# New priorities for a list-scheduled attention and mixture kernel

## The chip, the cores and the metric

The kernel runs on one core of a Trainium2 chip. The metric is device time in microseconds, the median of a few runs. The engines named here are TensorE (PE: matmuls and transposes), VectorE (DVE), ScalarE (ACT), GpSimd (POOL) and SyncE (SP, which issues the DMAs).

## The reference

The inputs are q, k and v for 8 batches, 8 heads, 576 positions and head size 64. For each head the scores q·kᵀ/8 are formed, every score below its row's maximum less tau (0.02) is dropped, the softmax of the rest is taken and multiplied by v. The heads of a batch together are x, 576 positions by 512 channels. Then:

```
theta = x @ w_theta
y = w_tok_r @ (x * cos(theta)) + w_tok_i @ (x * sin(theta))
u = x + y
out = u + relu(u @ w_ch)
```

w_theta and w_ch are 512 by 512, w_tok_r and w_tok_i are 576 by 576. Some weights come in 64-bit floats, and each weight is split into a high and a low 32-bit part; matmuls are done in three terms (high by high, high by low, low by high) to keep the precision.

## The kernel before, in words

**Tiling.** Heads are taken in pairs, 4 pairs to a batch and 32 in all. A pair has 9 *units* (288 in all, numbered h): 128 query rows of one head, or in the pair's first unit the last 64 rows of both heads. A unit is a chain over three engines. `score` (PE, L655) writes 128 by 576 scores into a PSUM tile of the kind "pair". `empty` (DVE, L670) scales them into a tile `sc` (4 of these exist) and takes the row extremum. `offset` (one small instruction) and `power` (ACT, the exponential, L691) follow. `mask` (DVE, L699) drops the small scores and sums the rows; it gives back the `sc` tile. `flip` (PE, L739) and `flip5` (L775) transpose the result, and `evict` (ACT, L750, L779) copies it out of PSUM. After the ninth unit `values` (PE, L823, 40 matmuls) multiplies by v, and `normalize` divides by the row sums, through a small DMA round trip (L865 to L883).

**The mixture.** When a batch has its four pairs, `mixture(b)` follows: `angle` (PE, L961, x by w_theta), `sines` (ACT, L1041), a multiplication on POOL (L1056; on DVE in the last batch), transposes (L1075), `token` (PE, L1123, the two token matrices, 216 matmuls), an addition (L1139), then the channel product (PE, L961 again, u by w_ch) and the store. It runs interleaved with the attention of the next batch; the last batch's mixture has nothing beside it.

**The weights.** At the start 13 pieces are loaded and split: 9 of the token matrices (576 wide, `weight_tok`) and 4 of w_theta (512 wide, `weight_mid`); 4 of w_ch follow after the first batch's scores. Each piece is one DMA, one ACT instruction (L348), five on DVE (L352, L356, L361, L366, L370), another on ACT (L375), matmuls into one or two banks (L399, L400) and ACT copies out (L403). Its tiles allow two pieces at a time. The token pieces are first read by `token(0)`, the w_theta pieces by `angle` of the first batch.

**What sets the order.** Nothing of this order is written out by hand. Every instruction, or small group of them, is a `Work` in a `Plan`: its engine, its modelled duration, what it needs, the buffers it takes, and a *rank*. When the program is built, `Plan.run` plays the whole list through. On the engine that can start something soonest it looks at all works that could start within a small slack of that moment (0.05 us on PE and POOL, 0.1 us on DVE and ACT, 0.8 us on SP) and takes the one with the lowest rank:

```
if first < NEVER and (best is None or first < best[0]):
    best = min((x for x in starts if x[0] <= first + SLACK[e]), key=lambda x: x[1].rank)
```

So the rank decides only between works that are ready together, and the program then issues each engine's instructions in the order found. A unit's rank is 3.2 h plus 3.2 times an entry of the table `LEAD`; in batch 0 the entry with a 0 behind its name is added (`score` and `score0`). A mixture's rank starts at 3.2 times 36 (b + 1), plus 3.2 times `mix`, and advances with its share of the mixture's matmuls. A token piece c has the rank 3.2 (`wk` + c `wk_step`), a w_theta piece 3.2 (`wt` + c `wt_step`). `prep` ranks the loads of q and k and their splitting, `wmload` the loads of the split w_theta and w_ch from DRAM. `split` is the time in us after which one of the two score tiles is given up for two more single banks. `angle`, `ztok`, `ztr`, `chan` and `span` set how fast a mixture's rank advances.

Of the kernel before, what the change touches and what calls it, by code (L numbers as in the profile page):

```python
# [39 lines left out]
SLACK = {"PE": 0.05, "DVE": 0.1, "ACT": 0.1, "POOL": 0.05, "SP": 0.8}  # L40

LEAD = dict(
    score=-4.72, empty=-32.86, offset=-8.97, power=-5.51, mask=15.23, flip=0.44, evict=-13.16, flip5=-0.53,
    values=1.44, vevict=-3.04, norm=-13.22, inv=-17.87, times=12.38, prep=-9.26, vload=3.1, mix=1.55, span=0.9,
    wt=0.48, wt_step=-10.83, wch=-3.05, wch_step=-0.24, wlow=14.42, xh=-17.5, xlast=15.0, angle=1.82, ztok=1.52,
    ztr=0.27, chan=0.95, aevict=4.03, wmload=6.36, absl=-8.83, sin=7.08, zmul=2.9, zev=-43.34, yev=-34.51, uh=-21.1,
    cev=-16.07, dma=1.13, hop=0.13, split=114.84, wk=-17.47, wk_step=-2.88, score0=-31.88, empty0=-6.42,
    offset0=15.77, power0=16.19, mask0=-7.4, flip0=-2.74, evict0=-0.54, flip50=-11.41, values0=-13.64,
    vevict0=-110.27, norm0=-7.09, prep0=-17.86, vload0=10.11, inv0=21.92, times0=17.78, mix0=-2.15, span0=0.08,
)  # L50


# [1211 lines left out]
```

## Time and profile before

| | us |
|---|---|
| median of 3 runs | 1006.82 |
| lowest, highest run | 1006.80, 1007.87 |
| span of the profiled execution, first to last instruction | 1003.4 |
| PE busy in it | 990.8 |
| DVE busy in it | 770.6 |
| ACT busy in it | 647.3 |
| POOL busy in it | 234.7 |

For the profiled execution only the span is listed, not its own time; the median lies 3.4 us above that span. The times of an engine are unions of its instructions. Those of PE are to be read with care: matmuls overlap each other and their ends are modelled, so a short wait may not show as idle time. The granted TensorE clock is full in every slice.

### The profile page before, as it was taken

To read this page: it belongs to the slowest core of one execution; us is meant where nothing else is said; L and a number is where in the kernel's file an instruction comes from. 1 tells how busy PE (TensorE), PEld (TensorE's weight loads), DVE (VectorE), ACT (ScalarE), POOL (GpSimd) and SP (SyncE) were. 2 spreads that over 40 slices of the span, in tenths; PEclk is the share of its full clock that TensorE was granted. 3 is DMA by queue.
4 is the path that set the end of the run, shared out by engine and by line. 5 is a ranking of instruction groups with operands and counts; after the bars stand their busy time and mean duration, and the time that the engine had idled before them with its cause. 6 is when DMAs were issued, how large, how long until landed. Compare 5 with 4: busy or idle time off the path is not lost.

```text
span 1003.4 us, 20961 instructions
## 1 busy us (share of the span) xinstructions
PE 990.8 (99%) x7574; PEld 890.5 (89%) x7574; DVE 770.6 (77%) x2038; ACT 647.3 (65%) x1292; POOL 234.7 (23%) x162
## 2 busy tenths in 40 slices
PE   9999999999999999999999999999999999999998
PEld 7766798998999989998999988999899989999898
DVE  7999978968866787767887688667887678876553
ACT  6898978645865568555775467755785457844430
POOL 2112132311342124222342113421242223400100
PEclk9999999999999999999999999999999999999999
DMA  7677946757534675437644575346853386441502
GB/s 227 201 208 193 245 154 170 201 150 218 163 88 101 189 218 133 118 72 231 183 126 103 144 203 166 98 107 164 236 141 90 85 241 188 110 92 34 174 22 69
DMA packets 86950, 151.89 MB, mean 151 GB/s; under 512 B 27200, under 2 KB 36672, under 8 KB 86848
## 3 DMA queue, kind: packets, MB, share of 16 engines
q1 hardware_dynamic: 86704, 150.56, 54.4%
q8 instruction: 60, 0.98, 0.4%
q14 instruction: 42, 0.34, 0.1%
q10 hardware_dynamic: 144, 0.00, 0.0%
HBM read 81.89 MB, written 13.78 MB: 95 GB/s over the span
## 4 chain that ended last, share of the span: by engine, by line
PE 91%; DVE 5%; issue 2%; DMA 1%; ACT 1%; SPq 0%; DVEq 0%; ACTq 0%
PE y_ps L1123 23%; PE m_ps L961 19%; PE o_ps L823 15%; PE s_ps L655 15%; PE t_ps L739 12%; PE z_ps L1075 3%; PE t_ps L775 2%; DVE s_sb L699 2%; DVE sc L670 1%; PE w_ps L399 1%; PE fill_ps L290 1%; DMA qraw<-in_qT_dram 0%; ACT a L750 0%; DMA wm<-wm_dram 0%; PE r_ps L854 0%
## 5 line engine op out<-in xcount | busy, mean ns | idle before, releaser
L670 DVE TENSOR_SCALAR_CACHE_REDUCE sc<-s_ps,small 128x576 f32<-128x576 f32 x288 | 234.0, 814 | 79.5 <-PE s_ps L655 78.2
L699 DVE SCALAR_TENSOR_TENSOR s_sb<-sc,nm,s_sb 128x576 f32<-128x576 f32 x288 | 241.7, 850 | 20.2 <-ACT s_sb L691 19.3
L691 ACT ACTIVATE s_sb<-sc,nm 128x576 f32<-128x576 f32 x288 | 222.6, 782 | 19.1 <-DVE sc L670 18.7
L750 ACT COPY a<-t_ps 128x512 f32<-128x512 f32 x256 | 150.3, 590 | 100.5 <-PE t_ps L739 99.3
L655 PE MATMUL s_ps<-kd,qq 128*128 128x288 f32 x992 | 179.1, 303 | 1.3 <-DVE sc L670 0.6
L739 PE MATMUL t_ps<-ident,s_sb 128*128 128x128 f32 x1152 | 173.3, 274 | 1.3 <-DVE s_sb L699 0.6
L1123 PE MATMUL y_ps<-wt_l,zh 128*128 128x288 f32 x576 | 166.6, 304 | 0.0
L1123 PE MATMUL y_ps<-wt_h,zh 128*128 128x288 f32 x576 | 166.4, 307 | 0.0
L823 PE MATMUL o_ps<-a,v 128*64 128x256 f32 (+1 forms) x1280 | 162.3, 408 | 0.0
L655 PEld LDWEIGHTS s_ps<-kd,qq 128*128 128x128 f32 x992 | 143.5, 188 | 7.0 <-DVE sc L670 5.5
L739 PEld LDWEIGHTS t_ps<-ident,s_sb 128*128 128x128 f32 x1152 | 137.1, 140 | 12.4 <-issue 7.9
L823 PEld LDWEIGHTS o_ps<-a,v 128*64 128x64 f32 x1280 | 89.1, 137 | 64.0 <-issue 3.9
L311 POOL TENSOR_TENSOR khl<-kraw,khl 128x576 fp32r<-128x576 f32 x31 | 47.3, 1526 | 325.1 <-ACT khl L551 206.5
L1056 POOL TENSOR_TENSOR z<-z,xT 128x576 f32<-128x576 f32 x56 | 78.2, 1431 | 138.0 <-ACT z L1041 138.0
L1123 PEld LDWEIGHTS y_ps<-wt_l,zh 128*128 128x128 f32 x576 | 108.2, 189 | 0.2
L1123 PEld LDWEIGHTS y_ps<-wt_h,zh 128*128 128x128 f32 x576 | 108.0, 189 | 0.3
L1123 PE MATMUL y_ps<-wt_h,zl 128*128 128x288 f32 x576 | 107.2, 298 | 0.0
L961 PE MATMUL m_ps<-xh,wm 128*128 128x288 f32 x512 | 97.4, 307 | 0.0
L961 PE MATMUL m_ps<-uh,wm 128*128 128x288 f32 x512 | 91.9, 302 | 0.9 <-DMA wm<-wm_dram 0.9
L1123 PEld LDWEIGHTS y_ps<-wt_h,zl 128*128 128x128 f32 x576 | 85.5, 188 | 0.4 <-issue 0.4
L834 ACT COPY xT<-o_ps 128x320 f32<-128x320 f32 x64 | 25.5, 398 | 93.3 <-PE o_ps L823 93.3
L961 PEld LDWEIGHTS m_ps<-xh,wm 128*128 128x128 f32 x512 | 75.5, 189 | 2.8 <-issue 2.7
(98 smaller groups left out, 1414.5 us busy)
## 6 DMA issues: line engine op xcount, KB each, us to landing
wm<-wm_dram SPq DMA_DIRECT2D x64, 512.0 KB
kd<-khl SPq DMA_DIRECT2D x62, 288.0 KB
qq<-qhl SPq DMA_DIRECT2D x124, 128.0 KB
kd<-khl SPq DMA_DIRECT2D x62, 256.0 KB
v<-in_vp_dram SPq DMA_DIRECT2D x32, 320.0 KB
kraw<-in_kT_dram SPq DMA_DIRECT2D x32, 288.0 KB
qraw<-in_qT_dram SPq DMA_DIRECT2D x32, 288.0 KB
rb<-rows_dram SPq DMA_DIRECT2D x64, 144.0 KB
```

The source lines that it names most:

```text
L311: eng.tensor_tensor(out=out, in0=a, in1=b, op=ALU.subtract)
L655: nc.tensor.matmul(ps.tile[:, half, to], st, kk[:, fr], start=(x == 0), stop=(x == len(terms) - 1))
L670: nc.vector.tensor_scalar(out=sc.tile.rearrange("p (a b) -> p a b", a=2), in0=ps.tile[:, :, :HS], scalar1=gate, scalar2=None, op0=ALU.mult ...
L691: nc.scalar.activation(out=u.s.tile[:, j], in_=sc.tile, func=AF.Exp, bias=nm.tile[:, 0:1], scale=-1.0)
L699: nc.vector.scalar_tensor_tensor(out=e, in0=sc.tile, scalar=nm.tile[:, 1:2], in1=e, op0=ALU.is_le, op1=ALU.mult, accum_out=pr.rows.tile[:, ...
L739: nc.tensor.transpose(out=bank.tile[:, c * P : (c + 1) * P], in_=sf[:, k0 + c * P : k0 + (c + 1) * P], identity=ident)
L750: nc.scalar.copy(out=t.a[:, :, j, q0 : q0 + P], in_=bank.tile.rearrange("p (c q) -> p c q", c=4))
L823: nc.tensor.matmul(bank.tile[64 * j : 64 * j + 64, :w], st, mv, start=(c == 0), stop=(c == 4))
L961: nc.tensor.matmul(banks[h].tile[:, :HS], wm.tile[:, a, c, :], x[:, h * HS : (h + 1) * HS], start=(key == 0), stop=(key == 11),)
L1056: eng.tensor_tensor(out=zi, in0=zi, in1=xs[m].x.tile, op=ALU.mult)
L1075: nc.tensor.transpose(out=bank.tile[:, i * P : (i + 1) * P], in_=z.tile[:, c : c + P], identity=ident)
L1123: nc.tensor.matmul(bank.tile[:, :HS], st, (wt_l if wl else wt_h)[:, c, hs], start=(k + q == 0), stop=(k + q == 26),)
```

## The change

Only the numbers of the table `LEAD` differ. The works, their needs, their modelled durations and their buffers are the same; the time at which the score tiles are split up (`split`) is one of the numbers.

```diff
 LEAD = dict(
-    score=-4.72, empty=-32.86, offset=-8.97, power=-5.51, mask=15.23, flip=0.44, evict=-13.16, flip5=-0.53,
-    values=1.44, vevict=-3.04, norm=-13.22, inv=-17.87, times=12.38, prep=-9.26, vload=3.1, mix=1.55, span=0.9,
-    wt=0.48, wt_step=-10.83, wch=-3.05, wch_step=-0.24, wlow=14.42, xh=-17.5, xlast=15.0, angle=1.82, ztok=1.52,
-    ztr=0.27, chan=0.95, aevict=4.03, wmload=6.36, absl=-8.83, sin=7.08, zmul=2.9, zev=-43.34, yev=-34.51, uh=-21.1,
-    cev=-16.07, dma=1.13, hop=0.13, split=114.84, wk=-17.47, wk_step=-2.88, score0=-31.88, empty0=-6.42,
-    offset0=15.77, power0=16.19, mask0=-7.4, flip0=-2.74, evict0=-0.54, flip50=-11.41, values0=-13.64,
-    vevict0=-110.27, norm0=-7.09, prep0=-17.86, vload0=10.11, inv0=21.92, times0=17.78, mix0=-2.15, span0=0.08,
+    score=-4.98, empty=-12.45, offset=-6.95, power=-1.14, mask=302.19, flip=0.97, evict=-106.74, flip5=0.33,
+    values=1.44, vevict=-44.01, norm=-20.15, inv=15.74, times=-60.18, prep=-6.6, vload=62.76, mix=1.4, span=0.9,
+    wt=-1.51, wt_step=-10.17, wch=11.16, wch_step=-14.85, wlow=-24.23, xh=-30.5, xlast=161.43, angle=1.743,
+    ztok=1.594, ztr=0.278, chan=0.926, aevict=-33.46, wmload=38.5, absl=56.98, sin=80.64, zmul=142.53,
+    zev=-188.21, yev=2.1, uh=-96.76, cev=-83.7, dma=1.13, hop=0.13, split=103.59, wk=-14.57, wk_step=2.97,
+    score0=-45.76, empty0=-58.68, offset0=17.08, power0=11.69, mask0=-60.05, flip0=-23.39, evict0=51.72,
+    flip50=-120.74, values0=102.45, vevict0=-21.98, norm0=-63.56, prep0=-20.42, vload0=-29.22, inv0=2.85,
+    times0=129.54, mix0=-0.37, span0=0.051,
 )
```

## Rows read from the trace of the kernel before

**Rows 1.** Stretches of the span: busy us (instructions) of each engine, clock, DMA.

```profile
17.00:117.00 100.00, 94.16 (x630) 70.79 (x630) 96.66 (x233) 90.23 (x216) 16.61 (x11) 1.00 0.75 208
...
117.00:144.70 27.70, 27.61 (x207) 24.01 (x207) 22.30 (x54) 21.04 (x46) 7.35 (x6) 1.00 0.64 172
...
125.00:875.00 750.00, 749.42 (x5872) 684.98 (x5871) 583.98 (x1586) 495.58 (x959) 203.84 (x137) 1.00 0.56 153
```

**Rows 2.** The chain of waits, later batches: start us, duration us, what.

```profile
289.93 5.00 PE o_ps L823 x40
...
407.38 5.00 PE o_ps L823 x40
...
524.89 5.00 PE o_ps L823 x40
...
600.11 4.83 DMA qraw<-in_qT_dram
...
643.05 5.00 PE o_ps L823 x40
...
760.61 5.00 PE o_ps L823 x40
```

**Rows 3.** Groups of DVE instructions, 17 to 117 us: count, busy us, mean ns, idle before.

```profile
L699 DVE SCALAR_TENSOR_TENSOR s_sb<-sc,nm,s_sb 128x576 f32<-128x576 f32 x40 | 34.1, 864 | 1.1 <-ACT s_sb L691 1.1
L670 DVE TENSOR_SCALAR_CACHE_REDUCE sc<-s_ps,small 128x576 f32<-128x576 f32 x42 | 33.6, 811 | 1.8 <-PE s_ps L655 1.4
L361 DVE SCALAR_TENSOR_TENSOR bits<-wraw,bits 128x576 uint32<-128x576 uint32 (+1 forms) x12 | 8.6, 715 | 0.1
L370 DVE SCALAR_TENSOR_TENSOR w<-wraw,mag 128x576 fp32r<-128x576 uint32 (+1 forms) x11 | 8.4, 768 | 0.0
L366 DVE TENSOR_SCALAR mag<-bits 128x576 uint32<-128x576 uint32 (+1 forms) x12 | 6.7, 559 | 0.0
L356 DVE TENSOR_SCALAR bits<-mag 128x576 uint32<-128x576 uint32 (+1 forms) x12 | 5.6, 466 | 0.0
L352 DVE TENSOR_SCALAR mag<-mag 128x576 f32<-128x576 f32 (+1 forms) x12 | 5.3, 441 | 0.7 <-ACT mag L348 0.3 <-ACT rinv L858 0.2
```

**Rows 4.** PE by time, weight pieces: start us, duration us, instruction.

```profile
10.05 0.65 PE L399 MATMUL w_ps<-bits,ident 128*128 128x288 f32 x2
...
11.55 0.39 PE L290 MATMUL fill_ps<-dummy 128*128 128x512 f32 x1
11.78 1.24 PE L655 MATMUL s_ps<-part,tails 128*128 128x288 f32 x6
...
83.88 0.29 PE L400 MATMUL w_ps<-wt_h,minus 128*128 128x288 f32 x1
...
101.86 0.40 PE L400 MATMUL w_ps<-whi,minus 128*128 128x512 f32 x1
...
116.85 0.51 PE L961 MATMUL m_ps<-xh,wm 128*128 128x288 f32 x2
...
144.71 0.30 PE L1123 MATMUL y_ps<-wt_h,zh 128*128 128x288 f32 x1
```

**Rows 5.** ACT by time, the first loads' readers.

```profile
6.23 0.72 ACT L348 ACTIVATE mag<-wraw 128x576 f32<-128x576 f32 x1 [3.79 <-DMA wraw<-in_w_tok_dram]
7.75 0.73 ACT L348 ACTIVATE mag<-wraw 128x576 f32<-128x576 f32 x1 [0.81 <-DMA wraw<-in_w_tok_dram]
```

**Rows 6.** DVE by time: the first scores, then three masks; in brackets idle time before.

```profile
15.64 0.82 DVE L699 SCALAR_TENSOR_TENSOR s_sb<-sc,nm,s_sb 128x576 f32<-128x576 f32 x1 [0.29 <-ACT s_sb L691]
...
17.03 0.82 DVE L670 TENSOR_SCALAR_CACHE_REDUCE sc<-s_ps,small 128x576 f32<-128x576 f32 x1 [0.56 <-PE s_ps L655]
...
32.82 1.87 DVE L699 SCALAR_TENSOR_TENSOR s_sb<-sc,nm,s_sb 128x576 f32<-128x576 f32 x1
...
34.62 0.81 DVE L699 SCALAR_TENSOR_TENSOR s_sb<-sc,nm,s_sb 128x576 f32<-128x576 f32 x1
...
96.53 1.99 DVE L699 SCALAR_TENSOR_TENSOR s_sb<-sc,nm,s_sb 128x576 f32<-128x576 f32 x1
```

**Rows 7.** POOL by time, around the first of those masks.

```profile
32.64 1.43 POOL L311 TENSOR_TENSOR qhl<-qraw,qhl 128x576 fp32r<-128x576 f32 x1
```

**Rows 8.** Waits of PE from 920 us on: total us, times, longest.

```profile
PE m_ps L961 <- DMA wm<-wm_dram: 0.9, 1, 0.9
PE z_ps L1075 <- DVE zl L311: 0.3, 1, 0.3
```

**Rows 9.** SP by time, near the end.

```profile
991.34 1.32 SPq L1188 DMA_DIRECT2D out_dram<-xT  x3
992.76 0.40 SPq L458 DMA_DIRECT2D wm<-wm_dram  x1
```

## The prediction

> **What bounds the kernel now.** I read first the stretches, then the chain of waits, then the groups of one engine in the stretch where the chain leaves PE, then the instructions by time. The stretches split the span in three. From 125 to 875 us PE is busy for 749.4 of 750 us, while DVE has 166 us of idle time and ACT 254 [rows 1]: the work of PE is the bound and whatever the others do in another order stays hidden, as long as something is ready for PE. The chain says the same by its rhythm: the 40 matmuls of `values` come back after one batch, 407.38 − 289.93 = 117.45 us, then 117.51, then 118.16, then 117.56 [rows 2]. One batch is 0.65 us slow; around it the chain runs through a load of q at 600 us, its only excursion to a DMA there. So the middle has nearly nothing to give.
>
> From 17 to 117 us it is otherwise: DVE is busy for 96.7 of 100 us and PE for 94.2 [rows 1], and DVE's few idle moments end on PE and ACT, 1.8 and 1.1 us [rows 3]. Here DVE is the bound. PE's true slack is larger than the 5.8 us shown, as a busy PE is not a full one, but what matters is DVE: it has 40 masks and 42 scalings to do, and beside them the twelve or so weight pieces [rows 3]. The last us are a third regime: PE alone, with 1.2 us of waits after 920 us, the largest 0.9 us on the load of a weight [rows 8].
>
> A change of 0.2% (2 us) is about what a measurement of this kernel can tell from none; "same" below means that.
>
> **The change part by part.** No instruction is added or removed, so every term is idle time, of PE in the middle and at the end, of DVE in the first stretch.
>
> *First loads.* In units of 3.2 per table entry, the ranks of the token pieces were −55.9 − 9.2c, so that piece 8 (−129.6) and 7 (−120.4) were ahead of the loads of pair 0 (−86.8). Now they are −46.6 + 9.5c, and only the last piece of w_theta (−102.5) is ahead of pair 0 (−86.5). The trace shows two token pieces read by ACT at 6.23 and 7.75 us before anything else, 1.52 us apart [rows 5], and the first score at 11.78 us [rows 4]. One load fewer before q and k moves the first score up by about 1.5 us. DVE gains only what it idles for then: 0.29 and 0.56 us around the first masks [rows 6], and about 0.15 us since the first piece is 512 wide, not 576 (an estimate: a ninth of 1.52). Term: −1.0 us. Ends: −1.5 if the whole advance is kept; +1.5 if DVE, with one weight piece instead of two to work on, is short of work for as long as one load takes.
>
> *Weight pieces later.* This is the largest term. Ranks on DVE in batch 0: scaling −125.7 + 3.2h, mask +25.1 + 3.2h before; −227.6 + 3.2h and +775 + 3.2h now. All token pieces now stand behind all 36 scalings of batch 0 (the last of these has −115.6), where most stood ahead of most. The masks are behind the weights in both. On PE the flips go from −7.4 + 3.2h to −71.7 + 3.2h, so they now pass many token pieces too. The order of the pieces also turns round. Before, the token pieces were finished at 83.9 us, though nothing reads them until `token` at 144.7, and the last w_theta piece came at 101.9, shortly before the first `angle` at 116.85, which needs it [rows 4]. After the change three of the four w_theta pieces are among the first five and the fourth (−4.8) is ninth; the end of the queue is token pieces 5 to 8 (+0.9 to +29.4). These may slip past the start of `angle`, and the work of batch 0 need not wait for them.
>
> A piece costs DVE 0.715 + 0.768 + 0.559 + 0.466 + 0.441 = 2.95 us [rows 3] and PE about 11.55 − 10.05 = 1.50 us [rows 4]. A piece that slips takes 2.95 us out of the DVE-bound stretch and puts 1.50 us of PE work into a stretch where PE is the bound: net −1.45 us. The cover for its DVE part is the stretch 117 to 144.7, where DVE idles for 5.4 us [rows 1]; that covers two pieces (5.9 us, nearly), not three. I take two: −2.9 us. Ends: 0 if the pieces run as soon as their two sets of buffers allow, which the masks' place behind them favours, and −5.8 for four pieces if the cover stretches to the following batch. If the cover is missing, `token` waits for a weight instead and the gain is gone.
>
> *Score tiles split earlier,* at 103.59 instead of 114.84 us. For 11 us, some four units (42 scalings in 100 us [rows 3]), a scaling must be over before the next score starts. A scaling that found no score ready had DVE idle for 0.56 us [rows 6]; four of these would be +2.2. Masks and weight work stand ready beside them, so I take 0; −0.5 is the other end, from the two more banks.
>
> *The middle.* Masks go from +48.7 to +967, behind everything on DVE; the copies of ACT (`evict`, `zev`) go to the front, the sines to the back (22.7 to 258); POOL's multiplications also (9.3 to 456); scores are 0.8 earlier and flips 1.7 later on PE. Each of these delays something by at most the instructions that pass it. With 22% of DVE and 34% of ACT idle, the masks still get through, and PE has the other stream, attention or mixture, to go on with. Value 0. Ends from the chain: −0.7 if the one slow batch becomes a normal one, and +4.2 if all seven batches pay the 0.6 us of that one [rows 2]. Who waits, if a mask is late: the flip, behind it on PE the flips of its pair, and the next `values`, as there is one set of tiles for the flipped scores.
>
> *SP.* The loads of the split weights fall from +20.4 to +123.2 behind the mixture's progress, so they are passed by loads, the moves of q and k and stores that become ready in the same 0.8 us. Each such issue takes about 0.4 us. Near the end the last of these loads already stood behind three stores, 991.34 to 992.76 us [rows 9], and PE waited 0.9 us for it [rows 8]. It cannot get better by this rank; 0, with ends 0 and +0.4 for one store more.
>
> Sum: −1.0 − 2.9 = −3.9, rounded to −4.0: a span of 999.4 us. The execution before lies 3.4 us over its span by the median, so the time is 1002.8 us.
>
> **The rivals.**
>
> *Nothing comes of it.* The weight pieces are paced by their two sets of buffers, which both versions have; ranks decide only between works that are ready together; no piece slips, and the −1.0 of the first loads is all: 1005.8 us, within the 2 us. For it: DVE idles 3% in the stretch, so the order there has little room. Against: the list of scalings that now goes ahead is long, and each piece needs five turns on DVE. 20%.
>
> *A larger gain.* Four pieces slip, the first loads keep 1.5 us, the slow batch goes: −5.8 − 1.5 − 0.7 = −8.0, 998.8 us. For it: 61 us lie between the last token piece and its first reader. Against: DVE's 5.4 us of cover. 16%.
>
> *Slower: masks meet POOL.* In the trace a mask that began at 32.82 us, inside a POOL subtraction that ran from 32.64 for 1.43 us, took 1.87 us; the next took 0.81 [rows 6, 7]. So a collision costs DVE 1.06 us, and two of the 11 POOL works of this stretch had one, the other at 96.53 us (1.99 us). The builder models this exclusion, with its own durations, and the new order shifts the masks, which are now whatever is left between other works, against POOL. Each further collision in the DVE-bound stretch adds 1.06 us to it; from the fourth on the forecast's gain is used up, and eight, nearly all that remain, give +8.5 − 4.0 = +4.5: 1011.3 us. The same side has the +4.2 of late masks in the middle if the gain in front fails too: 1011.0 us. Together 16%.
>
> The Trainium skill has this as a rule (SBUF — State Buffer, "Who interferes with whom"): a VectorE instruction with two SBUF inputs contends with a GpSimd instruction that reads SBUF, and the second to start blocks until the first is done. The 1.87 us fit it, since 34.07, the end of the subtraction, plus 0.81 would be 34.88 and the mask ended at 34.69.
>
> **How the numbers follow.** The forecast, faster by 2 to 6 us, has 48%; larger 16, nothing 20, slower 16. Some of the "nothing" reaches either side of 2 us, evenly. So faster 0.64, same 0.20, slower 0.16. The range leaves out the deepest gains and the dearest collisions: from 997.0 (the sum's terms at −8 and a little over) to 1009.0 us (half of the collisions, or the middle's end without the gain).
>
> **What would show it.** Right: the first score about 1.5 us sooner than 11.78; the w_theta pieces ready by 70 to 80 us and the last token pieces after 105; the first `angle` some 3 to 5 us before 116.85; the distance of `values` from batch to batch still 117.5; the end of the trace the same shape, 1 us of waits. Wrong: token pieces all done by 95 us (nothing slips); masks of 1.9 us in numbers before 117 us; batches of 118 us or more; or an `angle` at the old time with a shorter batch, which would say that the middle had a reserve that I do not see.

## The result, and the profile after

The changed kernel took 1012.83 us (median of 5 runs, 1010.84 to 1016.90) against 1006.80 us (5 runs): a ratio of 1.0066, 95% interval 1.0046 to 1.0085. It is slower by 6 us, where 4 us faster was forecast. The profiled execution took 1011.62 us with a span of 1009.8 us, 6.4 us more than before.

The stretches, in the columns of [rows 1]:

```profile
17.00:117.00 100.00, 91.46 (x607) 68.52 (x606) 98.30 (x225) 84.82 (x207) 17.38 (x11) 1.00 0.72 201
117.00:144.70 27.70, 27.29 (x212) 24.21 (x211) 21.94 (x55) 21.59 (x46) 8.41 (x6) 1.00 0.62 164
125.00:875.00 750.00, 746.39 (x5823) 680.50 (x5822) 606.69 (x1580) 498.08 (x954) 213.59 (x136) 1.00 0.57 154
```

Two things have changed. In the first stretch DVE is busy for 98.3 us in place of 96.7 although it finishes 225 instructions and not 233. In the middle DVE is busy for 22.7 us more with the same work, and PE has lost 3 of its 750 us. The same instructions have become longer.

The chain of waits, for [rows 2]:

```profile
294.54 5.00 PE o_ps L824 x40
...
412.83 5.00 PE o_ps L824 x40
...
531.16 5.00 PE o_ps L824 x40
...
629.64 2.72 DVE s_sb L700 x4
...
649.42 5.00 PE o_ps L824 x40
...
767.73 5.00 PE o_ps L824 x40
```

By the first of these the changed kernel is 4.6 us late (294.54 against 289.93 in [rows 2]). After that every batch but the last takes 118.3 us, where it was 117.5, and the chain now leaves PE once in each batch, for masks. The fourth, the eighth and the last of the 32 `values` tell where the time went (before, then after; a row breaks off where another instruction comes between):

```profile
108.28 2.10 PE L823 MATMUL o_ps<-a,v 128*64 128x320 f32 x14
232.58 3.77 PE L823 MATMUL o_ps<-a,v 128*64 128x320 f32 x28
934.52 5.07 PE L823 MATMUL o_ps<-a,v 128*64 128x320 f32 x40
```

```profile
107.00 3.34 PE L824 MATMUL o_ps<-a,v 128*64 128x320 f32 x24
235.18 1.03 PE L824 MATMUL o_ps<-a,v 128*64 128x320 f32 x6
942.04 2.37 PE L824 MATMUL o_ps<-a,v 128*64 128x320 f32 x16
```

The first batch is 1.3 us shorter, the second 3.9 longer, the six batches from the eighth to the last `values` 4.9 longer, and the rest 1.1 shorter, which adds up to the 6.4 us of the span. At the end PE's waits after 920 us, [rows 8], are now 0.4 us, and none is on a load.

The groups of DVE in the first stretch, for [rows 3] (lines are one later, since the table is one line longer):

```profile
L700 DVE SCALAR_TENSOR_TENSOR s_sb<-sc,nm,s_sb 128x576 f32<-128x576 f32 x42 | 35.9, 866 | 1.1 <-ACT s_sb L692 0.9
L671 DVE TENSOR_SCALAR_CACHE_REDUCE sc<-s_ps,small 128x576 f32<-128x576 f32 x40 | 31.8, 809 | 0.3
L371 DVE SCALAR_TENSOR_TENSOR w<-wraw,mag 128x576 fp32r<-128x576 uint32 (+1 forms) x11 | 9.2, 836 | 0.0
L357 DVE TENSOR_SCALAR bits<-mag 128x576 uint32<-128x576 uint32 (+1 forms) x10 | 8.1, 810 | 0.1
L362 DVE SCALAR_TENSOR_TENSOR bits<-wraw,bits 128x576 uint32<-128x576 uint32 (+1 forms) x10 | 7.8, 776 | 0.0
L367 DVE TENSOR_SCALAR mag<-bits 128x576 uint32<-128x576 uint32 (+1 forms) x10 | 6.9, 686 | 0.0
L353 DVE TENSOR_SCALAR mag<-mag 128x576 f32<-128x576 f32 (+1 forms) x10 | 4.3, 426 | 0.0
```

A weight piece costs DVE 0.836 + 0.810 + 0.776 + 0.686 + 0.426 = 3.53 us; it was 2.95. Over ten pieces that is 5.8 us. It comes from single instructions: in the first 117 us ten DVE instructions run longer than others of their line and shape by more than 0.2 us, 10.6 us in all, and each of them begins while GpSimd is inside a work. This is called a *meeting* below. Before the change there were six, 4.5 us in all.

What happens in a batch, DVE and then GpSimd and PE by time, for [rows 6, 7]:

```profile
629.63 0.81 DVE L700 SCALAR_TENSOR_TENSOR s_sb<-sc,nm,s_sb 128x576 f32<-128x576 f32 x1
...
630.36 1.99 DVE L700 SCALAR_TENSOR_TENSOR s_sb<-sc,nm,s_sb 128x576 f32<-128x576 f32 x1
...
632.29 0.81 DVE L671 TENSOR_SCALAR_CACHE_REDUCE sc<-s_ps,small 128x576 f32<-128x576 f32 x1
...
635.26 1.75 DVE L700 SCALAR_TENSOR_TENSOR s_sb<-sc,nm,s_sb 128x576 f32<-128x576 f32 x1
```

```profile
629.88 6.51 POOL L1057 TENSOR_TENSOR z<-z,xT 128x576 f32<-128x576 f32 x4 [6.66 <-ACT z L1042]
```

```profile
633.16 1.08 PE L656 MATMUL s_ps<-khl,tails 128*128 128x288 f32 x6 [0.49 <-DVE sc L671]
```

Three masks stand in a row. Before the third can start at 630.36, GpSimd has begun its four multiplications at 629.88. The mask takes 1.99 us in place of 0.81, the scaling behind it starts at 632.29, and PE, which has one score tile only, waits for that scaling before its next score. That wait of 0.49 us comes once in every batch from 278 us on, where there was none before. Over the kernel 27 masks of 288 took more than 1 us, and 10 did before; the mean went from 850 to 910 ns, 17 us in all. So the slower rival of the prediction is the suspect, in a place where it was not expected.

### The profile page after: what moved, and what is told of

Its sections match the earlier page's. It is cut to its first block, busy times and chain, and to the rows that moved or that the text cites. A ratio compares the mean times of both kernels' runs of the same rounds, so it can differ in the third digit from the quotient of the medians.

```text
span 1009.8 us, 20859 instructions
## 1 busy us (share of the span) xinstructions
PE 992.4 (98%) x7570; PEld 891.8 (88%) x7570; DVE 800.8 (79%) x2038; ACT 651.8 (65%) x1292; POOL 244.4 (24%) x162
## 4 chain that ended last, share of the span: by engine, by line
PE 85%; DVE 9%; ACT 2%; issue 2%; DMA 2%; SPq 0%; POOL 0%; POOLq 0%; DVEq 0%; ACTq 0%
PE y_ps L1124 20%; PE m_ps L962 19%; PE o_ps L824 14%; PE s_ps L656 14%; PE t_ps L740 11%; DVE s_sb L700 4%; PE z_ps L1076 3%; DVE sc L671 3%; PE t_ps L776 2%; PE w_ps L400 1%; PE fill_ps L291 1%; DMA wm<-wm_dram 1%; ACT s_sb L692 1%; DVE zl L312 1%; ACT zh L1082 0%
## 5 line engine op out<-in xcount | busy, mean ns | idle before, releaser
L700 DVE SCALAR_TENSOR_TENSOR s_sb<-sc,nm,s_sb 128x576 f32<-128x576 f32 x288 | 258.6, 910 | 9.7 <-ACT s_sb L692 8.3
L1124 PE MATMUL y_ps<-wt_h,zh 128*128 128x288 f32 x576 | 164.1, 308 | 0.0
L1057 POOL TENSOR_TENSOR z<-z,xT 128x576 f32<-128x576 f32 x56 | 86.7, 1579 | 86.5 <-ACT z L1042 86.5
```

The source lines that it names most:

```text
L700: nc.vector.scalar_tensor_tensor(out=e, in0=sc.tile, scalar=nm.tile[:, 1:2], in1=e, op0=ALU.is_le, op1=ALU.mult, accum_out=pr.rows.tile[:, ...
L1057: eng.tensor_tensor(out=zi, in0=zi, in1=xs[m].x.tile, op=ALU.mult)
L1124: nc.tensor.matmul(bank.tile[:, :HS], st, (wt_l if wl else wt_h)[:, c, hs], start=(k + q == 0), stop=(k + q == 26),)
```

## The experiments

*Theory P:* VectorE and GpSimd meet on a port, and the new order makes them meet more often. *Rivals:* the loss belongs to one part of the table alone (M, F); the masks' last place delays the score tiles, with or without a port (L); in the first stretch the order itself is slower (O). Each run is compared with the kernel before on the same chip, which took 1005.4 to 1006.9 us there.

**One part of the table at a time.** The entries named in the expectation were exchanged, for example in the first:

```diff
-    ... wt=0.48, wt_step=-10.83, ... split=114.84, wk=-17.47, wk_step=-2.88, score0=-31.88, empty0=-6.42,
+    ... wt=-1.51, wt_step=-10.17, ... split=103.59, wk=-14.57, wk_step=2.97, score0=-46.02, empty0=-38.27,
```

> The table of before, with the entries that set the first batch and the weights taken from the change (all names with a 0, so that the sums for batch 0 are the new ones, wt, wk, their steps, wch, wlow, split); later batches keep the old ranks. Theory P (VectorE and GpSimd meet on a port: in the first stretch more VectorE instructions run into GpSimd's, 10.6 us in place of 4.5, and from the second batch on masks run into the z multiplications): the first part alone costs what the end of the first mixture shows, 233.9 - 230.9 = +3.0 us, so about 1009.8 us, with batches of 117.5 us. Rival M (all of the loss is the middle, the first part is neutral): 1006.8 us. Rival F (all of it is the first part): 1012.8 us.

> The reverse: the changed table, with the first batch's sums and the weights' entries of before. Theory P: batches of 118.2 us from the second on as in the changed kernel, six of them +0.75 us, less 1.1 us at the end: +3.4, about 1010.2 us. Rival M: 1012.8 us. Rival F: 1006.8 us.

Measured: 1017.47 us (ratio 1.0111, 1.0096 to 1.0126) and 1020.67 us (1.0145, 1.0130 to 1.0160). Both missed, and by more than any of the theories allows: the halves do not add up. What they do tell is the place of the longer batch: `values` comes back after about 117.5 us with the old later entries and after 118.2 to 118.3 us with the new ones (659.82, 778.05 and 896.33 us in the second). Most of the rest is lost where the first batch hands over to the second; in the second kernel two neighbouring `values` lie at 153.1 and 215.3 us there. In the first kernel 4 us are lost before that as well (its first `angle` is at 120.9 us).

**The mask without its second input** (it compares and counts, and leaves out the product with the exponentials), in the same order of all engines, in the changed kernel and in the one before:

```diff
-            nc.vector.scalar_tensor_tensor(out=e, in0=sc.tile, scalar=nm.tile[:, 1:2], in1=e,
-                op0=ALU.is_le, op1=ALU.mult, accum_out=...)
+            nc.vector.tensor_scalar(out=e, in0=sc.tile, scalar1=nm.tile[:, 1:2], scalar2=None,
+                op0=ALU.is_le, op1=ALU.add, accum_out=...)
```

> The changed kernel in the very same order, but the mask reads one tensor and not two: it compares and counts, and leaves out the product with the exponentials. Theory P: masks of 1.8 to 2.0 us are gone (27 before), the wait of about 0.6 us for a score tile in each batch goes, batches are 117.5 us again: 1012.8 - 4.5 in the middle, and up to 2 us less in the first stretch, where two of the ten long VectorE instructions are masks: 1006 to 1008.5 us. Rival L (the masks' last place is what delays the score tiles, with or without the port): the batches stay at 118.3 us, 1012 us.

> The same edit in the kernel before, as its control: one long mask in each batch goes, and hardly one of them made PE wait. Theory P: 1005.5 to 1006.8 us. If the edit changes the time in itself (another duration of the mask), both this and the other move by the same amount; rival L expects that of the two, and no more.

Measured: 1002.91 us (0.9966, 0.9952 to 0.9981) and 1004.22 us (0.9988, 0.9977 to 0.9999). The edit takes 9.9 us from the changed kernel by the medians and 1.8 us from the other (by the ratios 10.0 and 1.2); both fell lower than expected. The mask's own length hardly differs (805 ns without a meeting, 812 before), no mask is long any more, batches are 117.5 us, and PE has no wait for a score tile after 125 us. Rival L is out: the masks still stand last. With this one instruction out of GpSimd's way, the new order is no longer the slower one. The weight pieces still meet GpSimd in this kernel (6.7 us in the first 117 us), and its first `angle` is at 114.05 us, 2 us before that of the changed kernel.

**GpSimd without reading:** memsets stand in for its multiplications by x, then for its subtractions too, so that the products and the low parts of q, k, x and u are left out; the third kernel is the control, the second edit in the kernel before.

```diff
-                        eng.tensor_tensor(out=zi, in0=zi, in1=xs[m].x.tile, op=ALU.mult)
...
+                        nc.gpsimd.memset(zi, 0.5)
+                        nc.gpsimd.memset(zi, 0.25)
...
-        eng.tensor_tensor(out=out, in0=a, in1=b, op=ALU.subtract)
+        if eng is nc.gpsimd:
+            eng.memset(out.bitcast(F32), 0.0)
+            eng.memset(out.bitcast(F32), 0.0)
...
```

> The changed kernel in the same order, the mask whole again, but GpSimd's multiplications of the mixtures (all but the last) are replaced by two memsets of the same tile each, so they read nothing; the product with x is left out. Theory P, narrow form (the masks that cost time in the middle are the ones that meet these multiplications): two of the four long masks of a batch go, the 0.6 us wait for a score tile goes, batches are 117.5 us in place of 118.3; 1012.8 - 4.5 = 1008.3 us, the first 117 us as in the changed kernel (first angle at 116). Rival P2 (the masks that meet the splitting of q, k, x and u do it): batches stay at 118.3, 1012 to 1013 us.

> As e5, and every subtraction on GpSimd (the low parts of q, k, x and u) is two memsets as well; the low parts are left out. No GpSimd instruction reads then. Theory P: no VectorE instruction of double length anywhere (10.6 us of them in the first 117 us of the changed kernel, 6.7 with the one-input mask), so the first angle comes 5 to 9 us before 116 us, batches are 117.5 us, and the time is 1012.8 - 4.5 - 5 to 8 = 1000 to 1003 us. Rival O (in the first stretch the order itself is slower, not the port): the first angle stays at 113 us or later, the time at 1004 us or above.

> The same edit as e6 in the kernel before, as its control: 4.5 us of long VectorE instructions in the first 117 us go. Theory P: first angle 3 to 4 us before 116.8, 1002 to 1004 us, so that the two orders differ by less than 2 us, the new one not slower. Rival O: the old order stays ahead by 3 us or more.

Measured: 1007.88 us (1.0026, 1.0011 to 1.0041), 998.51 us (0.9929, 0.9911 to 0.9947) and 1003.48 us (0.9978, 0.9969 to 0.9987). The direction is theory P's in all three, the sizes are not. The first is as expected: it brings the batches back to 117.55 us and leaves the first `angle` at 116.1, so the middle's loss is the masks that meet the multiplications (P2 is out). The second, 1.5 us below its expected range, moves the first `angle` from 116.02 to 109.97 us:

```profile
109.97 0.42 PE L966 MATMUL m_ps<-xh,wm 128*128 128x288 f32 x2
```

```profile
17.00:117.00 100.00, 97.05 (x657) 74.94 (x657) 96.07 (x237) 91.81 (x222) 12.00 (x20) 1.00 0.77 212
...
125.00:875.00 750.00, 750.00 (x5878) 686.14 (x5878) 574.74 (x1597) 501.18 (x962) 157.16 (x278) 1.00 0.56 153
```

These are the stretches of that kernel: PE busy for 97 of the 100 us from 17 to 117 where it was 91.5, with 50 matmuls more. In the control the first `angle` comes at 115.80, 1 us before its old place and not 3 to 4. So, with GpSimd reading nothing, the new order is the faster one by 0.9929/0.9978 = 0.9951, 4.9 us, where less than 2 was expected. The edit is worth 1.0066/0.9929 = 1.0138, 13.9 us, in the new order and 2.2 us in the old one.

Not all of that need be the port. A pair of memsets takes 1.16 us where a subtraction took 1.43, and a memset that reads nothing does not wait for its inputs either: GpSimd writes the low half of a `khl` at 53.94 us here, which in the changed kernel it computed at 60.17 us, when ACT's copy had come, and its readers can be served sooner.

```profile
60.17 1.45 POOL L312 TENSOR_TENSOR khl<-kraw,khl 128x576 fp32r<-128x576 f32 x1 [23.70 <-ACT khl L552]
```

```profile
53.94 0.58 POOL L313 MEMSET khl<- 128x576 f32 x1 [23.05 <-DMA kd<-khl]
```

In the changed kernel no wait of PE before 125 us ends on GpSimd or on a move of its results, which speaks for the port; but the chain of waits runs through a subtraction at 130.87 us, so for the handover that follows this is not shown. The kernels with the one-input mask are free of this doubt; and the memsets that stand in for the multiplications still wait for ACT's sines.

**Whole kernels that keep the two apart.** The multiplications on VectorE, planned anew; and the changed order as it is, with a copy of one column ahead of a GpSimd work, so that it waits for the VectorE instruction that the builder had put before it:

```diff
-                        eng = nc.vector if last else nc.gpsimd
+                        eng = nc.vector
...
```

```diff
+    def after_port():
+        if port[0] is not None:
+            nc.gpsimd.tensor_copy(out=seen_by_pool, in_=port[0]().bitcast(F32))
+            port[0] = None
...
+        def run():
+            after_port()
+            fn()
```

> A whole kernel: the changed table, with the multiplications of all mixtures on VectorE as in the last one, planned anew. 56 GpSimd works with 1.43 us each go, VectorE gets 56 of 0.75 us, 6 us per batch, against some 25 us of idle time. Theory P: the meetings at the multiplications are gone, batches of 117.5 to 117.9 us, 1007 to 1010 us if the new plan is no worse elsewhere (the plan changes as a whole, so some 5 us either way are open). Rival L (VectorE is too full for masks in last place): batches longer than 118.3 us, over 1013 us.

> A whole kernel: the changed order, unaltered, and ahead of each GpSimd work that the builder put behind a mask or a weight instruction of VectorE, GpSimd first copies one column of that instruction's output, so that it cannot start before it is over. The builder assumed that the two take turns; on the chip nothing made GpSimd wait. Theory P with this cause (GpSimd runs ahead of its turn): most of the 46 or so long VectorE instructions go, batches of 117.5 us, the first angle at 111 to 114 us, the time 1000 to 1006 us; faster than the changed kernel by 7 us or more. Rival W (the meetings come from VectorE being ahead or GpSimd late, or the waits cost GpSimd's readers as much): still 20 or more long ones, 1009 us or above.

> The same addition in the kernel before, as control: there are 17 long VectorE instructions and 2 us to win at most (the kernel without any reading on GpSimd took 1003.5). Theory P: 1003.5 to 1006 us; rival W: 1006 to 1008 us, the waits of GpSimd costing something.

Measured: 1010.37 us (1.0046, 1.0025 to 1.0066), 1006.16 us (1.0005, 0.9989 to 1.0020) and 1007.13 us (1.0007, 0.9996 to 1.0017). The first, just above its expected range, gets batches of 117.4 us with the masks still last, but the handover after the first batch is later (the second batch's `angle` at 246.3, 241.2 in the changed kernel). The second is clearer: with GpSimd made to wait, some 6 us of the loss are gone and the first `angle` is at 113.48, a little less than expected (1000 to 1006 us, a gain of 7 or more). Its control gained nothing and lies in the range of rival W, who held that the waits cost GpSimd's readers something; its first `angle` is at 118.11, 1.3 us later than without the waits. In the middle of the second kernel:

```profile
628.32 0.18 POOL L307 COPY seen_by_pool<-rows 128x1 f32<-128x1 f32 x1 [7.68 <-DVE s_sb L715]
628.45 4.20 POOL L1073 TENSOR_TENSOR z<-z,xT 128x576 f32<-128x576 f32 x3
633.41 0.19 POOL L307 COPY seen_by_pool<-rows 128x1 f32<-128x1 f32 x1 [0.76 <-DVE s_sb L715]
633.54 1.44 POOL L1073 TENSOR_TENSOR z<-z,xT 128x576 f32<-128x576 f32 x1
```

GpSimd waits 7.68 us for the mask, then runs three multiplications, waits 0.76 us for another mask, and runs the fourth: the turns that the builder had planned. Where GpSimd is in the middle of a work when the mask comes, nothing holds the mask back, and masks of 1.4 us remain (44 VectorE instructions still run long by over 0.2 us, 51 in the changed kernel; their excess went from 54 to 28 us). So the count of long instructions is as rival W said, and their sum and the time are nearer to theory P. In the first stretch the excess hardly fell, 10.6 to 9.0 us: in all ten meetings there the GpSimd work was already running when the VectorE instruction began, and the copy holds only GpSimd back.

**The builder told of longer GpSimd works:** 1.39 replaced by 1.50 and by 1.65 us in the modelled durations of e9, with the same table.

> A whole kernel: e9, and the builder is told that a GpSimd work lasts 1.50 us in place of 1.39 (the chip takes 1.43 and the copy ahead of it), so that it keeps the masks off for as long; planned anew with the changed table. Theory P: fewer long VectorE instructions than the 44 of e9, batches of 117.5, and the time between that of e9 (1006) and that without meetings (998.5): 1001 to 1005 us. Rival C (the table's numbers fit only the plan that they were found with): any new plan with it is worse than e9, 1008 us or above, whatever the meetings.

> The same with 1.65 us, about the 1.43 and 0.22 that the trace of e9 shows for a subtraction and the copy before it. Theory P: as e11 or better, 1000 to 1005 us. Rival C: 1008 us or above.

Measured: 1019.25 us (1.0135, 1.0109 to 1.0160) and 1022.35 us (1.0183, 1.0158 to 1.0208). Rival C came true in both. The last has nearly no long instruction after 235 us (4, where the changed kernel has 36) and late batches of 117.4 us, and yet it is the slowest of all: the second batch's `angle` begins at 258.8 us. No version that I ran beats both kernels with the whole computation.

## Why the prediction was wrong, by its own steps

Two steps failed. The weight term took VectorE's instructions to keep their lengths (2.95 us a piece), and they came out at 3.53, which over ten pieces ate all that the two slipped ones had freed; and the middle, priced at 0, cost 4.9 us. The runs put both down to meetings with GpSimd, the second by two separate edits.

*First loads: right in kind.* The first score came at 9.62 us, 2.2 us earlier, where 1.5 was forecast.

*Weight pieces later: this step failed in its price; its mechanism was right.* Two token pieces slipped, as I had taken, but past the end of the cover: their matmuls lie at 157.6 to 162.1 us. The 5.9 us that this freed on VectorE went to the ten pieces that stayed, 0.58 us longer each. So the first `angle` came 0.8 us earlier, not 3 to 5, while the work moved on: the second batch is 3.9 us longer, and two slipped pieces are 3.0 us of it by the 1.50 us of the sum. With GpSimd reading nothing `angle` came 6 us earlier than that. The new order is then ahead of the old one by 4.8 us at the fourth `values` (102.50 against 107.25) and by 2.6 at the eighth (228.08 against 230.69), where the sum had 3.9. That the two times differ by 4.9 us, near the 4.0 forecast, is in part luck: 1.7 us of the difference come after the last `values`, where the sum had 0.

*Score tiles split earlier:* PE's waits for a scaling before 125 us rose from 0.6 to 5.1 us, but of the four only one, 1.29 us at 113.95, comes after the split, so this term stayed inside its end of +2.2. The other three come before it, behind meetings. Here a long weight instruction at 33.56 makes the scaling late, and PE waits:

```profile
33.56 1.64 DVE L357 TENSOR_SCALAR bits<-mag 128x512 uint32<-128x512 uint32 x1
35.12 0.80 DVE L671 TENSOR_SCALAR_CACHE_REDUCE sc<-s_ps,small 128x576 f32<-128x576 f32 x1
```

```profile
35.99 0.79 PE L656 MATMUL s_ps<-kd,qq 128*128 128x288 f32 x4 [1.29 <-DVE sc L671]
```

With GpSimd reading nothing, PE has no wait for a scaling left before 125 us.

*The middle: this step failed.* I priced it at 0, since VectorE has idle time there and PE another stream to go on with. Its upper end, 4.2 us, was near the right size: 0.8 us in each batch, 4.9 us in all. An average of idle time says nothing of a single late scaling that PE's only score tile waits for.

*SP:* priced 0, as a rank that could not make the end better; the rest after the last `values` is 1.1 us shorter. In the batch before it, though, the chain runs through a load of a weight at 813.62 us, and PE waits 0.3 us for one.

*The rival that came true* had the right price (1.06 us for a meeting; 1.18 and 0.94 us in the batch shown) and the wrong place: the masks of the first stretch met GpSimd twice, as before, while the weight instructions there did so oftener, and 25 masks did later, where 8 had. Of its two forms, eight meetings of masks in the first stretch (1011.3 us) did not come; late masks in the middle with the gain in front gone (1011.0 us) came, through meetings. The Trainium skill's rule (SBUF — State Buffer, "Who interferes with whom") has both: two SBUF inputs against a reading GpSimd, which agrees with masks that are short with one input (805 ns); and `tensor_scalar` in a form without an accumulator, which agrees with the L357 and L367 of the first stretch. I had read it for masks alone, and so counted two meetings in the first stretch of the kernel before where the trace has six, such as this one, which is 0.42 us elsewhere:

```profile
87.05 1.64 DVE L366 TENSOR_SCALAR mag<-bits 128x512 uint32<-128x512 uint32 x1
```

I also took it that the builder's model of the exclusion holds on the chip. [Rows 6, 7] held the counter-evidence: a meeting in the old kernel, which the builder would never have planned. The model orders each engine; it makes no engine wait.

Of the signs set beforehand, the earlier first score and the last token pieces after 105 us came. The last w_theta piece was ready at 89 us, not by 70 to 80, and the batches of 118 us were named as a sign of being wrong.

## What to carry to other kernels

A plan that assumes that two engines take turns at a port loses that wherever one engine runs ahead, unless a wait in the program holds it back; and a wait on one side alone, as here, gives only part of it back. Look in the trace for the same instruction of the same shape at two lengths before trusting the plan. Priorities belong to one plan: with half of the table exchanged, or a modelled duration changed by 8% or 19%, the kernels took 11 to 17 us longer than the one before. Price a reordering with what it puts next to what, not with the idle time of the engines.

## What the runs showed of the hardware

A scalar operation with a single SBUF input was stretched too:

```profile
62.16 1.65 DVE L357 TENSOR_SCALAR bits<-mag 128x576 uint32<-128x576 uint32 x1
```

```profile
61.57 1.93 POOL L312 TENSOR_TENSOR qhl<-qraw,qhl 128x576 fp32r<-128x576 f32 x1
```

It is 0.45 us elsewhere. The scalings, which read PSUM and accumulate, never were: their mean is 809 to 816 ns everywhere. Against a GpSimd that only writes, the masks stayed short (812 ns), and a few scalar operations and casts still ran 0.2 to 0.4 us long, 10 of them and 3.3 us in all in the changed order. This one began inside the memset shown above, at 53.94 us, and takes 0.46 us alone:

```profile
54.02 0.81 DVE L361 TENSOR_SCALAR bits<-mag 128x576 uint32<-128x576 uint32 x1
```

TensorE's clock was not always full. Of the changed kernel's five runs, the two with a mean granted clock of 1.000 took 1010.84 and 1011.62 us, those with 0.998 took 1012.83 and 1013.69, and the one with 0.992 took 1016.90. In the profile of the kernel with the added waits (mean 0.998) the lower level, 1.2 GHz, stands in the first attention units:

```profile
14.00:16.00 2.00, 2.00 (x13) 1.43 (x12) 2.00 (x6) 1.38 (x4) 0.14 (x1) 1.00 0.83 232
16.00:18.00 2.00, 1.99 (x14) 1.75 (x13) 2.00 (x7) 2.00 (x5) 0.00 (x0) 0.84 1.01 196
18.00:20.00 2.00, 2.00 (x7) 1.31 (x7) 2.00 (x4) 1.13 (x4) 1.30 (x2) 0.50 0.96 227
20.00:22.00 2.00, 2.00 (x9) 1.13 (x8) 2.00 (x6) 1.89 (x6) 0.24 (x1) 0.80 0.87 223
```

PE is shown busy throughout before and during the fall, with 7 matmuls in the 2 us at 0.50. The profile of the changed kernel has 1.00 in the same stretch, so its 6.4 us of span hold none of this; the median's last us or two may. Which stretch fell in the run with 0.992 is not shown.
